# Two 256-token blocks joined into one of 512 in both MLP layers, from block 4 on, with a new order for the head

## The chip, the cores and the metric

The kernel runs on one core of one Trainium2 chip, as one launch. The metric is the device time of that core in microseconds (us); less is better. The median of three runs of the kernel before is 944.13 us.

The engines are named as the profile names them: PE is TensorE (PEld its weight loads), DVE is VectorE, ACT is ScalarE, POOL is GpSimd, SP is the engine that issues the DMAs. "n" in a PE row is the count of columns that stream through it.

## The reference

Attention over keys and values that are averaged in groups of 8, then two matrix products with a rational function between them. 8 sequences of 576 tokens give 4608 rows of 512 features.

```python
k_p = k.reshape(B, H, Sp, 8, D).mean(axis=3)       # B=8, H=8, Sp=72, D=64
v_p = v.reshape(B, H, Sp, 8, D).mean(axis=3)
scores = np.matmul(q, k_p.transpose(0, 1, 3, 2)) / np.sqrt(D)
attn = softmax(scores)
x = np.matmul(attn, v_p)                            # -> (4608, 512)
h = x @ w_in                                        # 512 -> 2048
P = a[0] + a[1]*h + a[2]*h**2 + a[3]*h**3
Q = 1.0 + abs(b[0])*abs(h) + abs(b[1])*h**2
out = (P / (Q + 1e-6)) @ w_out                      # 2048 -> 512
```

The weights come as 64-bit floats and are read as two 32-bit words each.

## The kernel before

**Work.** The 4608 rows are 18 blocks of 256 tokens (`TOK`). The 2048 hidden features are 8 units of 256 (`NU`). For a block, `attend(i)` makes x: scores (tiles `ps`), softmax (`mx`, `e`, `sm`), the transposed probabilities (`am`), and the product with the pooled values (`pv`, in two halves, which ACT copies to x's high part and DVE subtracts to x's low part). `prep_k` and `prep_v` pool the keys and values of a sequence first (`st`, `ks`, `pk`, `pl`, `kpT`; `vs`, `vm`, `vr`; for the first two sequences on PE as `pvs` and `pvr`).

**Each product in three.** Every operand of the two layers is split into a high part and a low part, and a product is high by high, low by high, high by low. For a block and a unit, `mm1` issues 24 matmuls of 256 columns into one PSUM bank `ph`: two halves of the unit's features, three products, four chunks of the 512 features. `rational` turns `ph` into `gh` and `gl` with 13 instructions: ACT `w`, `t`, `r`; POOL `w`; DVE `t` twice (the second is the last reader of `ph`); ACT `rp` twice; DVE `t`, `rp`, `t`; ACT `gh`; POOL `gl`. `mm2` adds 12 matmuls of 512 columns to two banks `po`, one for each half of the block's tokens. PSUM has eight banks, all of one pool: two `po`, the others for `ph`, `rp` (the rational function's scratch) and the attention.

**Weights.** `load_weights` brings 1 MB for a unit of one layer (`rwin`, `rwout`), ACT and DVE rebuild floats from the words in a scratch tile `m`, ACT copies the high part, POOL subtracts the low part. All 16 stay in SBUF. Until unit weights arrive their places hold the first sequences' keys and values (`early`).

**Order.** Nothing runs in the order in which it is written. Each instruction is added to a `Plan` with an engine, a cost and a due time (`plan.now`); `solve` then lists the instructions by a model of engine, port, DMA and buffer times, and `issue` writes them out. Each engine runs its list in order; semaphores make it wait where an operand is late. Where the model sees PE idle, `issue` puts in filler matmuls (256 columns, tile `idle`, or `po<-zero`). Blocks 0 to 3 come first, mixed, while the weights arrive: units 0 to 3 of blocks 0 and 1, all of 2 and 3, then units 4 to 7 of blocks 0 and 1, whose x is written out to HBM (`xd`) and read again. Then block by block, unit by unit. `SHIFTS` are seeds of random offsets on the due times of the first 1850 instructions.

## Time and profile before

| | |
|---|---|
| runs | 943.72, 944.13, 944.32 us |
| span of the profiled execution, first to last instruction | 943.9 us |
| PE, PEld, DVE, ACT, POOL busy | 99%, 90%, 83%, 73%, 56% of the span |
| matmuls `ph` (256 columns), `po` (512 columns) | 3456, 1728 |
| DMA | 75.33 MB, mean 80 GB/s; 275, 313, 390 GB/s in the first three fortieths |
| granted TensorE clock | 1.00 |

The page gives no time of the profiled execution other than its span; the span lies between the lowest and the highest of the three runs, 0.2 us under their median, so a change of the span is taken as a change of the time. A busy share is the time in which an engine had at least one instruction; matmuls overlap, so their own lengths add to more than the span, and the step from one to the next is what they cost.

### The profile page before, as it was taken

What the parts mean: (1) busy time and instruction counts of PE and PEld (TensorE: products, weight loads), DVE (VectorE), ACT (ScalarE), POOL (GpSimd) and SP (SyncE); (2) the same over time, 40 slices, a digit from 0 to 9 for tenths busy, and PEclk for the clock granted to TensorE, in tenths of its full rate; (3) what the DMA queues carried; (4) which work ended last, traced back from release to release, by engine and by line L of the source; (5) the groups of instructions that cost most, each with busy time, mean ns of one, the idle gap of its engine ahead of it and who ended that gap; (6) DMA issues with size and microseconds to landing.
All of it is one profiled execution on the core that took longest, in us unless ns stands there. A gap on an engine that the chain in (4) does not pass through costs nothing.

```text
span 943.9 us, 17079 instructions
## 1 busy us (share of the span) xinstructions
PE 932.3 (99%) x6152; PEld 845.0 (90%) x6152; DVE 786.0 (83%) x1336; ACT 693.7 (73%) x1124; POOL 528.0 (56%) x463
## 2 busy tenths in 40 slices
PE   8899999999999999999999999999999999999998
PEld 8888998989988899998999899998999899999996
DVE  7799988788989888887887997888898987887664
ACT  4788889868675877686776777676868595868674
POOL 4776866866446544445634574447545663544443
PEclk9999999999999999999999999999999999999999
DMA  9994201254235322122603160316222421202000
GB/s 275 313 390 160 45 29 46 67 127 87 49 81 105 86 34 47 29 56 53 138 5 75 51 140 8 54 37 139 47 36 50 97 50 28 51 1 57 1 23 23
DMA packets 185365, 75.33 MB, mean 80 GB/s; under 512 B 162624, under 2 KB 162624, under 8 KB 185280
## 3 DMA queue, kind: packets, MB, share of 16 engines
q1 hardware_dynamic: 185280, 74.23, 31.2%
q8 instruction: 49, 0.80, 0.4%
q14 instruction: 36, 0.29, 0.1%
HBM read 50.60 MB, written 12.58 MB: 67 GB/s over the span
## 4 chain that ended last, share of the span: by engine, by line
PE 87%; DMA 3%; SPq 3%; DVE 3%; POOL 1%; ACT 1%; issue 1%; POOLq 0%; ACTq 0%
PE ph L284 39%; PE po L284 39%; PE pv L284 4%; PE ps L284 4%; SPq L284 3%; DMA q<-in_q_dram 1%; DMA early<-in_v_dram 1%; DVE sm L284 1%; DMA st_v<-in_v_dram 1%; DVE t L284 1%; POOL w L284 0%; PE pvs L284 0%; ACT rp L284 0%; PE pq L284 0%; DVE mx L284 0%
## 5 line engine op out<-in xcount | busy, mean ns | idle before, releaser
L284 PEld LDWEIGHTS ph<-x,win 128*128 128x128 f32 x3264 | 472.7, 188 | 55.5 <-ACT w L284 0.8
L284 PE MATMUL ph<-x,win 128*128 128x256 f32 x3264 | 495.7, 282 | 1.4 <-DVE x L284 0.5
L284 PE MATMUL po<-wout,gh 128*128 128x512 f32 x1152 | 353.1, 397 | 0.1
L284 POOL TENSOR_TENSOR w<-w,r 128x512 f32<-128x512 f32 (+1 forms) x145 | 191.1, 1318 | 230.3 <-ACT r L284 228.1
L284 POOL TENSOR_TENSOR gl<-t,gh 128x512 fp32r<-128x512 f32 (+1 forms) x145 | 193.3, 1333 | 93.1 <-ACT gh L284 91.9
L284 PEld LDWEIGHTS po<-wout,gh 128*128 128x128 f32 x1152 | 185.7, 189 | 12.5 <-POOL wout L284 0.8
L284 PE MATMUL po<-wout,gl 128*128 128x512 f32 x576 | 181.8, 396 | 0.3 <-POOL gl L284 0.3
L284 ACT ACTIVATE rp<-w,cbias 128x512 f32<-128x512 f32 (+1 forms) x145 | 99.6, 687 | 59.8 <-POOL w L284 56.6
L284 DVE SCALAR_TENSOR_TENSOR t<-t,abn,rp 128x512 f32<-128x512 f32 (+1 forms) x145 | 107.3, 740 | 38.4 <-ACT rp L284 35.3
L284 DVE TENSOR_TENSOR t<-t,ph 128x512 f32<-128x512 f32 (+1 forms) x145 | 97.8, 675 | 48.7 <-ACT t L284 46.7
L284 ACT ACTIVATE r<-w,abn 128x512 f32<-128x512 f32 (+1 forms) x145 | 117.9, 813 | 20.8 <-POOL gl L284 11.4
L284 ACT ACTIVATE t<-ph,abn 128x512 f32<-128x512 f32 (+1 forms) x145 | 111.0, 767 | 26.3 <-PE ph L284 23.0
L284 ACT ACTIVATE w<-ph 128x512 f32<-128x512 f32 (+1 forms) x145 | 85.7, 591 | 40.8 <-PE ph L284 34.4
L284 DVE SCALAR_TENSOR_TENSOR t<-t,abn,ph 128x512 f32<-128x512 f32 (+1 forms) x145 | 107.0, 738 | 5.2 <-ACT w L284 1.3
L284 ACT CAST gh<-t 128x512 fp32r<-128x512 f32 (+1 forms) x145 | 88.3, 609 | 20.5 <-DVE t L284 16.9
L284 DVE SCALAR_TENSOR_TENSOR t<-rp,t 128x512 f32<-128x512 f32 (+1 forms) x145 | 99.4, 685 | 4.1
L284 DVE SCALAR_TENSOR_TENSOR rp<-w,rp 128x512 f32<-128x512 f32 (+1 forms) x145 | 99.0, 683 | 0.2
L284 PEld LDWEIGHTS po<-wout,gl 128*128 128x128 f32 x576 | 93.0, 189 | 6.4 <-POOL gl L284 0.5
L284 ACT ACTIVATE rp<-rp 128x512 f32<-128x512 f32 (+1 forms) x145 | 84.1, 580 | 3.6 <-DVE t L284 0.5
L284 POOL TENSOR_TENSOR e<-e,sm 128x576 f32<-128x576 f32 x36 | 41.8, 1175 | 51.2 <-DVE sm L284 38.7
L284 POOL TENSOR_TENSOR st_v<-st_v 128x512 f32<-128x512 f32 (+1 forms) x36 | 36.3, 1015 | 17.4 <-DMA st_v<-in_v_dram 10.7
L284 PE MATMUL ps<-kpT,qT 128*128 128x144 f32 (+1 forms) x320 | 45.6, 292 | 0.4 <-DVE kpT L284 0.2
(101 smaller groups left out, 855.9 us busy)
## 6 DMA issues: line engine op xcount, KB each, us to landing
am<-e SPq DMA_DIRECT2D x224, 48.0 KB, 2.1
out_dram<-ob SPq DMA_DIRECT2D x17, 512.0 KB, 3.1
rwin<-in_moe_w_in_dram SPq DMA_DIRECT2D x8, 1024.0 KB, 11.1
rwout<-in_moe_w_out_dram SPq DMA_DIRECT2D x8, 1024.0 KB, 14.1
st_k<-in_k_dram SPq DMA_DIRECT2D x12, 512.0 KB, 4.8
st_v<-in_v_dram SPq DMA_DIRECT2D x12, 512.0 KB, 4.2
q<-in_q_dram SPq DMA_DIRECT2D x144, 32.0 KB, 2.0
st_v<-in_v_dram SPq DMA_DIRECT2D x48, 64.0 KB, 2.2
```

The lines of the kernel that those rows point to most:

```text
L284: getattr(engines[op.eng], name)(*map(value, args), **{k: value(v) for k, v in kw.items()})
```

## The change

From block 4 on, blocks i and i+1 go through both layers as one of 512 tokens. `mm1_wide` takes one half of a unit's features (128) and both blocks' tokens: 12 matmuls of 512 columns into one bank `ph`. So `u` now counts to 16 for a pair, and `ph`, `t`, `w`, `r`, `gh`, `gl` keep their size. `mm2_wide` adds to four banks `po`, 128 tokens each, instead of two. x lies in one tile `X` with three places for a block; a pair has two of them, and the next pair's first block is attended into the third while the pair runs.

SBUF room for that comes from dropping the pools `stage` and `dec`: weights are decoded in the places of later weights (or in `near` and `far`, two tiles of 1024 columns), and keys, values and outputs are staged in halves of `near` and `far`, so keys, values and outputs move in pieces half as large (769 DMA issues on SP instead of 676; 480 tensor-tensor instructions on POOL instead of 420, 382 on DVE instead of 351). The four and the two coefficients are no longer sent to 128 partitions by DMA; they land on one partition and a matmul (`ab`) spreads them.

The planner's model gets new constants (an engine is free before its result can be read: `TAIL`, `HOP`; lower costs for DVE, ACT and POOL), it tracks parts of tiles through more kinds of views (`box`, `covers`), and instead of random offsets two tables (`LATER`: 154 entries on due times, `HOLD`: 74 earliest starts) shape the order.

```diff
-    LAT = 0.07
+    TAIL = {"sp": 0.0, "pe": 0.16, "pool": 0.06, "dve": 0.09, "act": 0.1}
+    HOP = {"sp": 0.035, "pe": 0.035, "pool": 0.08, "dve": 0.035, "act": 0.035}
...
-    SHIFTS = (600170, 650652, 293686, 721265, 222299, ...
+    LATER = {
+        40: -31199.3, 45: -9979.2, 50: -7560.7, 61: -7094.9, 66: -1347.5, 67: -1073.3,
...
+    HOLD = {
+        71: 22.46, 76: 23.98, 104: 14.67, 116: 22.44, 138: 34.87, 316: 59.14, 458: 31.17, 461: 53,
...
-    dve = Engine(plan, "dve", 0.16, 1.04)
-    act = Engine(plan, "act", 0.17, 0.85)
-    gp = Engine(plan, "pool", 0.45, 1.72)
+    dve = Engine(plan, "dve", 0.068, 1.04)
+    act = Engine(plan, "act", 0.06, 0.85)
+    gp = Engine(plan, "pool", 0.14, 2.15)
...
+    X = new("cpool", "x", [P, 3, 2, NJ, TOK], F32R, "x")
+    near, far = (new("cpool", x, [P, 2 * DM], F32, x) for x in ("in", "out"))
+    taken = {near.tile: 0, far.tile: 0}
+
+    def half(x):
+        n = taken[x.tile] = taken[x.tile] + 1
+        return x[:, n % 2 * DM:(n % 2 + 1) * DM]
...
     def scalars():
-        dma(2, ab[:, 0:4], a.partition_broadcast(P))
-        dma(1, ab[:, 4:6], b.partition_broadcast(P))
+        small("memset", line, 1.0)
         for i in range(4):
-            small("tensor_scalar", out=abn[:, i:i + 1], in0=ab[:, i:i + 1],
-                                scalar1=-WS ** -i, scalar2=None, op0=ALU.mult)
-        act(6).activation(abn[:, 4:6], ab[:, 4:6], AF.Abs)
+            small("memset", scale[:, i:i + 1], -WS ** -i)
+        dma(0.02, ab[:, 0:4], a.unsqueeze(0))
+        dma(0.02, ab[:, 4:6], b.unsqueeze(0))
+        every = bank("ab", [P, 6])
+        pe(220, [mm(every, line, ab, True, True)])
...
-        m = new("dec", "m", [P, CW], F32, f"m_{name}")
+        if u >= NA:
+            m = near if kind == "win" else far
+        else:
+            if kind == "win" and not decoding:
+                decoding.append(new("cpool", "win6", [P, 2 * CW], F32, "m6"))
+            m = (decoding[0] if kind == "win" else early(0, 0))[:, u % 2 * CW:(u % 2 + 1) * CW]
...
+    def slot(i):
+        place_of[i] = i % 2 if i < 4 else (2, 0, 1)[i % 3 - 1]
+        return [X[:, place_of[i], s] for s in range(2)]
...
+    def mm1_wide(i, u):
+        ph = bank(f"ph{i}_{u}", [P, 2, TOK])
+        w, f, n = weights["win", u // 2], u % 2, DM // P
+        lo, hi = sorted((place_of[i], place_of[i + 1]))
+        last = read[-PHS:-PHS + 1] if PHS > 1 else read[-1:]
+        for s, (wi, xi) in enumerate(((0, 0), (1, 0), (0, 1))):
+            last = pe(231.6 * n, [
+                mm(ph, w[:, wi, (2 * c + f) * P:(2 * c + f + 1) * P],
+                   X[:, lo:hi + 1:hi - lo, xi, c, :], s == 0 and c == 0, s == 2 and c == n - 1)
+                for c in range(n)], after=last),
+        return ph
...
+    def mm2_wide(i, u, gh, gl):
+        if u == 0:
+            pos[i] = [bank(f"po{i}_{m}", [P, DM]) for m in range(4)]
+        w = weights["wout", u // 2][:, :, u % 2 * DM:(u % 2 + 1) * DM]
...
+        high, low = ((gh, 0), (gh, 1)), ((gl, 0),)
+        if not final:
+            for terms in (high, low):
+                for m in range(4):
+                    products(m, terms)
+            return
+        tail = last(i, u)
+        for h in range(2):
+            for n in range(2):
+                m = 2 * h + n
+                plan.now += 5.0 * tail
+                products(m, high)
+                products(m, low)
+                row = (i + (h ^ swap)) * TOK + n * P
+                ob = half(near if tail and h else far)
+                evict(n, ob, pos[i][m])
+                dma(256, out[row:row + P, :], ob)
...
-    order += [(i, u) for i in range(4, NBLK) for u in range(NU)]
+    order += [(i, u) for i in range(4, NBLK, 2) for u in range(2 * NU)]
```

What the planner makes of it is seen in the engines' lists. SP's list in the head, first before (the two coefficient loads, `ab`, stand ahead of the second pair of q tiles, `q1`, which tokens 256 to 511 need):

```order
L284 DMA q0_109<-in_q_dram 128x8x64 x2
L284 DMA early0_2_116<-in_v_dram 128x4x512
L284 DMA rwin0_121<-in_moe_w_in_dram 128x4x512
L284 DMA early0_1_103<-in_v_dram 16x2x512 x2
L284 DMA rwin1_145<-in_moe_w_in_dram 128x4x512
L284 DMA ab_177<-in_moe_b_dram 128x2
L284 DMA ab_177<-in_moe_a_dram 128x4
L284 DMA rwout0_214<-in_moe_w_out_dram 128x2x1024
L284 DMA q1_256<-in_q_dram 128x8x64 x2
```

and now (`fourfold` is the tile in which the coefficients land; `early1_2` is the second sequence's values, 1 MB):

```order
L341 DMA early0_2_114<-in_v_dram 128x4x512
L341 DMA rwin0_121<-in_moe_w_in_dram 128x4x512
L341 DMA early0_1_109<-in_v_dram 16x2x512
L341 DMA rwin1_134<-in_moe_w_in_dram 128x4x512
L341 DMA early0_1_109<-in_v_dram 16x2x512
L341 DMA fourfold_140<-in_moe_b_dram 1x2
L341 DMA early1_1_196<-in_k_dram 64x512
L341 DMA rwin2_215<-in_moe_w_in_dram 128x4x512
L341 DMA q1_250<-in_q_dram 128x8x64 x2
L341 DMA rwout1_277<-in_moe_w_out_dram 128x2x1024
L341 DMA early1_2_314<-in_v_dram 128x4x512
```

The 128-row loads of a and b are gone from ahead of `q1`; a third `rwin` stands there in the place of the first `rwout`, with 128 KB of keys.

PE's list in the head, before, from the last transpose of block 0's probabilities (`pr`) to the first product with the values (`pv`); `pq2` transposes a tile of `q1`:

```order
L284 MATMUL pr1_344<-identr_83,e0_240 128x128 x2
L276 MATMUL idle_101<-identr_83 128x256 x22
L284 MATMUL idle_101<-identr_83 128x128
L284 MATMUL pq2_390<-identr_83,q1_256 128x128 x4
L284 MATMUL pv0_0_397<-am0_0_340,vm00_302 128x256
L284 MATMUL pv0_0_397<-am0_0_340,vm10_305 128x256
```

and now, from the product that pools the first values on:

```order
L341 MATMUL pvs0_257<-early0_2_114,identr_76 128x256 x8
L333 MATMUL idle_101<-identr_76 128x256 x16
L341 MATMUL pm0_308<-identr_76,e0_243 128x128 x4
L341 MATMUL pvr0_318<-early0_1_109,fourfold_140 128x128 x8
L341 MATMUL pr0_339<-identr_76,e0_243 128x128 x2
L341 MATMUL pm1_342<-identr_76,e0_243 128x128 x4
L341 MATMUL idle_101<-identr_76 128x128
L341 MATMUL pr1_362<-identr_76,e0_243 128x128 x2
L341 MATMUL pq3_370<-identr_76,q1_250 128x128 x4
L341 MATMUL pv0_0_379<-am0_0_336,vm00_283 128x256
```

The block of 22 fillers before `pq` is gone, 16 stand further up; a transpose of `q1` still stands ahead of the first `pv`.

PE's list in the later part, before, in block 8 (first and second layer alternate, four matmuls of 256 columns and two of 512):

```order
L284 MATMUL ph8_7_5829<-x0_8_5273,win7_1856 128x256 x4
L284 MATMUL po8_0_0_5598<-wout4_1973,gh8_4_5826 128x512
L284 MATMUL po8_0_1_5600<-wout4_1973,gh8_4_5826 128x512
L284 MATMUL ph8_7_5829<-x0_8_5273,win7_1856 128x256 x4
L284 MATMUL po8_0_0_5598<-wout4_1973,gh8_4_5826 128x512
```

and now, where the pair of blocks 8 and 9 ends and that of 10 and 11 begins (the row above this piece is the last `pv11_1`, which makes half of block 11's x):

```order
L341 MATMUL po8_0_5295<-wout7_2036,gl8_15_6180 128x512
L341 MATMUL po8_1_5301<-wout7_2036,gl8_15_6180 128x512
L341 MATMUL po8_2_5304<-wout7_2036,gh8_15_6168 128x512 x2
L341 MATMUL ph10_0_6248<-x_396,win0_332 128x512 x12
L341 MATMUL ph10_1_6273<-x_396,win0_332 128x512 x12
L341 MATMUL ph10_2_6304<-x_396,win1_410 128x512 x4
L341 MATMUL po8_3_5309<-wout7_2036,gh8_15_6168 128x512 x2
L341 MATMUL po8_2_5304<-wout7_2036,gl8_15_6180 128x512
L341 MATMUL po8_3_5309<-wout7_2036,gl8_15_6180 128x512
L341 MATMUL ph10_2_6304<-x_396,win1_410 128x512 x8
L341 MATMUL ph10_3_6339<-x_396,win1_410 128x512 x12
L341 MATMUL po10_0_6372<-wout0_654,gh10_0_6365 128x512 x2
```

Two matmuls of 256 columns have become one of 512, and at a pair's end the first layer of the next pair runs while the last sums of the old one are still open.

More of the change, by code (lines that the diff above doesn't have):

```diff
@@ L54, in box @@
     def box(self):
+        box = [(0, n) for n in self.tile.shape]
+        whole, axes = list(box), list(range(len(box)))
         for name, args, _ in self.chain:
@@ L59, in box, with covers @@
             if name != "__getitem__":
-                return ()
+                break
             idx = args[0] if isinstance(args[0], tuple) else (args[0],)
-            out = []
-            for i, n in zip(idx, self.tile.shape):
-                out.append((i, i + 1) if isinstance(i, int) else
-                           (i.start or 0, n if i.stop is None else i.stop))
-            return tuple(out)
-        return ()
+            left = []
+            for n, d in enumerate(axes):
+                lo, hi = box[d]
+                i = idx[n] if n < len(idx) else slice(None)
+                if isinstance(i, int):
+                    box[d] = lo + i, lo + i + 1
+                else:
+                    left.append(d)
+                    box[d] = (lo + (i.start or 0), hi if i.stop is None else lo + i.stop)
+                    if i.step and i.step > 1:
+                        box[d] = box[d][0], box[d][1] - (box[d][1] - box[d][0] - 1) % i.step
+            axes = left
+        return () if box == whole else tuple(box)
 def meet(a, b):
     return all(x0 < y1 and y0 < x1 for (x0, x1), (y0, y1) in zip(a, b))
+def covers(a, b):
+    return not a or b and all(x0 <= y0 and y1 <= x1 for (x0, x1), (y0, y1) in zip(a, b))
 class Buf:
@@ L230, in solve @@
                 op.end = t + 2 * op.cost
+            op.done = op.end + self.TAIL[op.eng]
             at[op.eng] = op.end
@@ L333, in tile_pooled_attention_then_rational_moe @@
     LAG = 4
+    PHS = 2
     NA = NU // 2
@@ L491, in prep_k @@
         pl = bank(f"pl{n}", [P, P])
-        for c0, c1, np in ((0, 2, P), (2, 4, P), (4, 5, H * SP - 4 * P)):
+        for c0, c1, np in ([(0, 2, P), (2, 4, P)] if n < 2 else [(c, c + 1, P) for c in range(4)]
+                           ) + [(4, 5, H * SP - 4 * P)]:
             nc_ = c1 - c0
@@ L496, in prep_k @@
             else:
-                place = new("stage", "st", [P, 1024], F32, f"st_k{n}_{c0}")[:, 0:nc_ * RW]
+                place = half(near)
             dma(2 * np * nc_, place[:np].rearrange("p (c x) -> p c x", c=nc_),
@@ L562, in prep_v @@
         vrs = vs_all[:, NJ * D:(NJ + 2) * D].rearrange("p (c d) -> p c d", d=D)
-        for c in (2, 0, 1):
-            place = new("stage", "st", [P, 1024], F32, f"st_v{n}_{c}")
-            st = place.rearrange("p (j x) -> p j x", j=2)
-            if c < 2:
-                dma(512, st, rows[2 * c:2 * c + 2, REM:, :].rearrange("j r x -> r j x"))
+        for c in (4, 5, 0, 1, 2, 3):
+            place = half(near)
+            if c < 4:
+                dma(256, place, rows[c, REM:, :])
             else:
@@ L656, in attention @@
         sm = new("work2", "sm", [P, H], F32, f"sm{t}")
+        scores = [bank(f"ps{t}_{c}", [P, 4, SP]) for c in range(2)]
+        calls = [mm(scores[c][r0:r1, 2 * jj:2 * jj + 2, :], qT[:, 2 * c + jj, r0:r1],
+                    kpT[n % 2][:, 2 * c + jj, :], True, True)
+                 for c in range(2) for jj in range(2) for r0, r1, n in sg]
+        for part in [calls] if len(sg) > 1 else [calls[:2], calls[2:]]:
+            pe(1350 if len(sg) > 1 else 244 * 2, part, claims=(e, mx, sm))
         for c in range(2):
@@ L659, in attention @@
             js = slice(2 * c, 2 * c + 2)
-            ps = bank(f"ps{t}_{c}", [P, 4, SP])
-            pe(245 * 2 * len(sg), [
-                mm(ps[r0:r1, 2 * jj:2 * jj + 2, :], qT[:, 2 * c + jj, r0:r1],
-                   kpT[n % 2][:, 2 * c + jj, :], True, True)
-                for jj in range(2) for r0, r1, n in sg], claims=(e, mx, sm))
+            ps = scores[c]
             dve(4 * SP).tensor_reduce(out=mx[:, hs], in_=ps, op=ALU.max, axis=AX.X)
@@ L777, in reload @@
     def reload(i, kept):
-        xs = [new("work2", f"x{s}", [P, NJ, TOK], F32R, f"xr{s}_{i}") for s in range(2)]
+        xs = slot(i)
         for x, d in zip(xs, kept):
@@ L845, in products @@
                 for m in ms], claims=[pos[i][m] for m in ms])
-        if last(i, u):
-            for m in range(2):
-                plan.now += 10.0 * m
-                for n in range(6):
-                    products(n, (m,))
-                ob = new("dec", "m", [P, DM], F32, f"ob{i}_{m}")
-                evict(m, ob, pos[i][m])
-                dma(256, out[i * TOK + m * P:i * TOK + (m + 1) * P, :], ob)
-            return
         for n in range(6):
@@ L915, in tile_pooled_attention_then_rational_moe @@
                 plan.now = due(at)
-        if ("win", u) not in weights:
+        if i < 4 and ("win", u) not in weights:
             load_weights("win", u)
@@ L922, in tile_pooled_attention_then_rational_moe @@
         gh, gl = rational(i, u, ph)
-        if ("wout", u) not in weights:
+        if i < 4 and ("wout", u) not in weights:
             load_weights("wout", u)
```

156 lines of the change are left out of this document (93 added, 63 removed), and 32 rows, old and new, of tables (HOLD, LATER).

## The prediction

> **What bounds the kernel now.** I read the page's first lines, then the busy time by windows, then the chain of work that ended last, PE's waits, and the timelines of PE and SP in the head.
>
> ```profile
> span 943.9 us, 17079 instructions
> PE 932.3 (99%) x6152; PEld 845.0 (90%) x6152; DVE 786.0 (83%) x1336; ACT 693.7 (73%) x1124; POOL 528.0 (56%) x463
> ```
> ```profile
> 0.00:25.00 25.00, 21.66 (x143) 19.76 (x143) 18.12 (x41) 11.22 (x22) 12.08 (x52) 1.00 0.88 264
> 25.00:50.00 25.00, 22.56 (x177) 21.30 (x178) 19.28 (x36) 19.27 (x36) 20.48 (x17) 1.00 1.06 333
> 50.00:75.00 25.00, 24.81 (x172) 22.06 (x172) 22.81 (x40) 21.04 (x33) 17.94 (x10) 1.00 1.04 396
> 500.00:600.00 100.00, 100.00 (x669) 90.56 (x668) 86.18 (x151) 72.33 (x119) 53.95 (x45) 1.00 0.30 67
> ```
>
> The windows (start:end, length, then busy time of PE, PEld, DVE, ACT, POOL, clock, DMA share, GB/s) tell two stages apart. From about 40 us on PE is never without work; the clock is 1.00, DMA is at 0.30. There only fewer or shorter matmuls, or a new wait, can move the end. In the first 50 us the 16 DMA engines are full (0.88, 1.06) and PE has gaps: a start that waits for data.
>
> What a matmul costs is read from unbroken pieces of the chain (start, length, count):
>
> ```profile
> 125.43 1.89 PE ph L284 x16
> 149.82 2.86 PE ph L284 x24
> 174.69 2.38 PE ph L284 x20
> ...
> 227.62 1.83 PE po L284 x8
> ...
> 382.15 1.88 PE pv L284 x16
> ...
> 928.99 11.15 PE po L284 x48
> ```
>
> A `ph` of 256 columns takes 118.1, 119.2, 119.0 ns, together 7.13 / 60 = 118.8; a `po` of 512 columns 228.8 and, over 48, 232.3; a `pv` of 256 columns 117.5.
>
> **The change, part by part.**
>
> *Wide first layer.* Blocks 4 to 17 have 14 x 192 = 2688 `ph` of 256 columns; they become 1344 of 512. Taking a `ph` of 512 columns at the step of a `po`, each saves 2 x 118.8 - 232.3 = 5.3 ns: 1344 x 5.3 = 7.1 us, all on the path. Bounds: by the cheapest 256-column row (`pv`, 117.5) 2.7 ns, 3.6 us; by the dearest `ph` and the cheapest `po` (119.2, 228.8) 9.6 ns, 12.9 us; if the step goes by columns alone, nothing. I take the long `po` row, since it has the new shape and 48 samples. The second layer keeps 1728 `po` of 512 columns: nothing.
>
> [...]
>
> *The head.* PE's list has a transposition of q (`pq`) ahead of the first `pv`; the list now too.
>
> ```profile
> 21.02 2.87 PE L276 MATMUL idle<-identr 128*128 128x256 f32 x22
> 23.73 0.39 PE L284 MATMUL idle<-identr 128*128 128x128 f32 x2
> 25.60 0.63 PE L284 MATMUL pq<-identr,q 128*128 128x128 f32 x4 [1.49 <-DMA q<-in_q_dram]
> ```
> ```profile
> 12.02 13.45 DMA q<-in_q_dram
> ```
> ```profile
> 18.00:20.00 2.00, 2.00 (x19) 1.88 (x19) 1.58 (x4) 0.92 (x4) 1.15 (x1) 1.00 0.63 241
> ...
> 22.00:23.00 1.00, 1.00 (x10) 1.00 (x10) 0.99 (x3) 1.00 (x3) 0.00 (x0) 1.00 0.82 196
> 23.00:24.00 1.00, 1.00 (x10) 0.93 (x8) 0.97 (x2) 1.00 (x3) 0.00 (x0) 1.00 0.44 95
> 24.00:25.00 1.00, 0.12 (x2) 0.00 (x0) 0.97 (x3) 0.31 (x1) 0.61 (x1) 1.00 0.42 62
> ```
>
> PE did 22 fillers and then waited 1.49 us for the second pair of q tiles, which was issued at 12.02 and landed at 25.47. In that stretch the DMA engines were not full: 0.37 x 2 + 0.18 + 0.56 + 0.58 = 2.1 us of their time went unused, around the 128-row loads of `ab`, which stand right ahead in SP's list. Those go; ahead of q now stands the same number of megabytes (a `rwin` for a `rwout`, and 128 KB more). So q should land about 2.1 us sooner, and the gate with it. Bounds: nothing, if the unused time has another cause or block 0's probabilities come later than now; 2.87 + 1.49 = 4.4 us, all fillers and the wait. I take 2.1.
>
> Behind the gate PE waits for small things, up to 100 us:
>
> ```profile
> PE ph L284 <- DVE x L284: 0.5, 1, 0.5
> PE pm L284 <- POOL e L284: 0.4, 1, 0.4
> PE pk L284 <- POOL ks L284: 0.4, 1, 0.4
> PE pv L284 <- DVE am L284: 0.3, 1, 0.3
> ...
> PE pq L284 <- issue: 0.2, 1, 0.2
> ```
> ```profile
> L276 PE MATMUL po<-zero,identr 128*128 128x256 f32 x10 | 1.7, 282 | 0.0
> ```
>
> These four waits and the `pq` make 1.8 us, and ten fillers of 118.8 ns 1.2. The new list puts 40 `ph` between the scores of block 1 and the transposes that need them, where `pm` and `ph` waited, and has no filler in this stretch. But the second sequence's values (`pvs1`) are now wanted some 7 us after the gate, when their 1 MB, issued behind 8 MB, has hardly landed at the 333 to 396 GB/s above. I take half of the waits and the fillers: 0.9 + 1.2 = 2.1 us less. Bounds: 3.0 less, 2 more.
>
> *The end.* Before, the last unit's `ph` was written and read by halves in one bank:
>
> ```profile
> 926.79 0.74 PE L284 MATMUL ph<-x,win 128*128 128x256 f32 x4 [0.39 <-ACT w L284]
> ...
> 928.25 0.74 PE L284 MATMUL ph<-x,win 128*128 128x256 f32 x4 [0.25 <-ACT t L284]
> ```
>
> A wide `ph` is read only when whole: these waits, 0.6 us, go. After it stand 48 `po` as before. Output stays two 256 KB pieces at the end: nothing.
>
> *New waits between pairs.* At a pair's start nothing of its own can fill PE until the first `gh` is there. Its chain, by the means of the groups:
>
> ```profile
> L284 ACT ACTIVATE w<-ph 128x512 f32<-128x512 f32 (+1 forms) x145 | 85.7, 591 | 40.8 <-PE ph L284 34.4 <-DVE t L284 6.1
> L284 ACT ACTIVATE r<-w,abn 128x512 f32<-128x512 f32 (+1 forms) x145 | 117.9, 813 | 20.8 <-POOL gl L284 11.4 <-DVE rp L284 1.9
> L284 POOL TENSOR_TENSOR w<-w,r 128x512 f32<-128x512 f32 (+1 forms) x145 | 191.1, 1318 | 230.3 <-ACT r L284 228.1 <-PE ph L284 1.6 <-PE ps L284 0.7
> L284 ACT ACTIVATE rp<-w,cbias 128x512 f32<-128x512 f32 (+1 forms) x145 | 99.6, 687 | 59.8 <-POOL w L284 56.6 <-DVE am L284 0.9 <-DVE kpT L284 0.8
> L284 ACT ACTIVATE rp<-rp 128x512 f32<-128x512 f32 (+1 forms) x145 | 84.1, 580 | 3.6 <-DVE t L284 0.5
> L284 DVE SCALAR_TENSOR_TENSOR t<-t,abn,rp 128x512 f32<-128x512 f32 (+1 forms) x145 | 107.3, 740 | 38.4 <-ACT rp L284 35.3 <-DVE t L284 0.5
> L284 DVE SCALAR_TENSOR_TENSOR rp<-w,rp 128x512 f32<-128x512 f32 (+1 forms) x145 | 99.0, 683 | 0.2
> L284 DVE SCALAR_TENSOR_TENSOR t<-rp,t 128x512 f32<-128x512 f32 (+1 forms) x145 | 99.4, 685 | 4.1
> L284 ACT CAST gh<-t 128x512 fp32r<-128x512 f32 (+1 forms) x145 | 88.3, 609 | 20.5 <-DVE t L284 16.9 <-PE ph L284 2.9
> L284 ACT ACTIVATE t<-ph,abn 128x512 f32<-128x512 f32 (+1 forms) x145 | 111.0, 767 | 26.3 <-PE ph L284 23.0 <-DVE rp L284 2.4 <-POOL w L284 0.5
> L284 DVE TENSOR_TENSOR t<-t,ph 128x512 f32<-128x512 f32 (+1 forms) x145 | 97.8, 675 | 48.7 <-ACT t L284 46.7 <-ACT w L284 1.7
> L284 DVE SCALAR_TENSOR_TENSOR t<-t,abn,ph 128x512 f32<-128x512 f32 (+1 forms) x145 | 107.0, 738 | 5.2 <-ACT w L284 1.3
> ```
>
> The first nine add to 6.7 us. Behind one other unit on ACT (its six instructions, 4.0 us) it is 10.7. At the start of pair 10 the list has 36 `ph` and 4 `po` between the end of `ph10_0` and the first use of its `gh`, 40 x 232.3 ns = 9.3 us; the like places at other pairs' starts and ends, by the same count, have 8.2 (the end of the first pair) to 18 us. So each of the six transitions loses between nothing and about 2 us, 0 to 12 in all. I take 0.3 each, 1.9 us, near the lower end, because a chain that meets a free engine is nearer to 6.7; and the nine fillers that the list has at the end of the first pair, 1.1. Sum 3.0.
>
> *At nothing:* the third place in `X` (block i+2's x is copied while the pair still runs; if it comes late, `ph` of the next pair waits for it, behind it all of PE); 93 more issues on SP and 60 more instructions on POOL, since POOL is busy 56% and keys and values are pooled a pair ahead (if that cover is gone, `kpT` is late and `ps` waits); weights decoded in one or two scratch places (the units that use them come later than their landing).
>
> **The sum.** 943.9 - 7.1 - 2.1 - 2.1 - 0.6 + 3.0 = 935.0 us of span. The median of the runs is 0.2 above the span: 935.2.
>
> **The rivals.**
>
> *Too few banks (slower).* Four banks now hold `po`, so four are left for `ph`, `rp`, `ps` and `pv`, where there were six. A `ph` bank is free when DVE has read it twice: 0.591 + 0.813 + 0.767 + 0.675 + 0.738 = 3.6 us after the last matmul when ACT does `r` before `t`, and 4.8 with two more instructions of 0.6 us ahead (the next x is copied at that time). In 16 places of the list a `ph` begins 2.8 to 4.2 us, 3.5 on average, after the end of the one two before it (pair 10: 12 x 232.3 = 2.8). If that bank is the only one, a place loses 4.8 - 3.5 = 1.3 us: 20 us, 955. From 0.7 us a place the kernel is slower. For it: PE's list has nothing else there. Against: at those places the old pair's four sums are just being given back, so a third bank is often free.
>
> *The head gains nothing:* full DMA engines (1.06) or a later transposition set the gate anyway. 935.2 + 2.1 + 2.1 = 939.4. For it: the shares of 1.04 to 1.06 up to 75 us.
>
> *A smaller fixed cost per matmul:* by the `pv` row 3.6 in place of 7.1 us, 938.7. [...] By columns alone the first layer saves nothing: 942.3.
>
> *More is gained:* transitions lose only the fillers (1.9 less) and the gate moves by 4.4 (2.3 less): 931.0.
>
> **How the numbers follow.** Forecast 935.2, chance 0.52, its own range 933 to 938; head without gain 0.15; smaller fixed cost 0.10; more gained 0.13; columns alone 0.03; banks 0.07. About 0.2% of the time, 1.9 us, is what can be told from no change. The first four are faster: 0.90. Columns alone, and the mild part of the banks, within 0.2%: 0.04. Slower: 0.06. From 930.5 to 941 lie the forecast, the small fixed cost, nearly all of the head and half of the gains: 0.82.
>
> **What would show it.** Right: chain pieces of the new `ph` near 232 ns; `pq` or the first `pv` at about 23.5 us; no `DMA q` wait of 1.5; windows from 100 us on with PE within 0.3 us of full per 50; no waits of `ph` for ACT at the end. Wrong: waits of PE `ph` for DVE `t` or of `po` for ACT `gh` that sum to over 8 us at the pairs' starts (banks or transitions); a `ph` of 237 ns; `pq` still at 25.6.

## The result, and the profile after

The changed kernel takes 954.71 us (median of four runs, 953.26 to 956.76) against 943.98 for the kernel before in the same job: a ratio of 1.0115 [1.0101, 1.0128], 10.7 us slower, where 8.9 us less was forecast. The device time lies 1.7 us above the span for runs of before and 1.9 for runs of after, not 0.2: by this difference the profiled execution of before, with its span of 943.9 us, took some 945.6 us, more than any of the four runs of before (943.72 to 944.32).

The page of after opens with these lines (compare the 932.3 us of PE in 6152 matmuls before):

```profile
span 954.8 us, 14586 instructions
PE 932.8 (98%) x4796; PEld 776.1 (81%) x4796; DVE 778.0 (81%) x1367; ACT 695.5 (73%) x1124; POOL 535.9 (56%) x532
```

Busy time by windows of after (start:end, length, PE, PEld, DVE, ACT, POOL, clock, DMA share, GB/s):

```profile
25.00:50.00 25.00, 24.89 (x185) 24.27 (x186) 21.34 (x39) 20.58 (x34) 17.13 (x14) 0.93 1.06 358
500.00:600.00 100.00, 97.81 (x465) 78.56 (x464) 86.74 (x158) 70.31 (x114) 53.10 (x54) 1.00 0.32 67
```

The second 25 us are now nearly full (24.89 us of PE; 22.56 before), at a mean clock of 0.93. In the steady stretch from 500 to 600 us PE lacks 2.2 us where it lacked nothing. Much of the loss is in the part without a data wait.

The chain of work that ended last (page, part 4, shares of the span), before:

```profile
PE 87%; DMA 3%; SPq 3%; DVE 3%; POOL 1%; ACT 1%; issue 1%; POOLq 0%; ACTq 0%
```

and after:

```profile
PE 45%; DVE 22%; ACT 9%; SPq 7%; POOL 6%; issue 5%; DMA 5%; DVEq 0%; ACTq 0%; POOLq 0%
```

PE carried 87% of the chain; now it carries 45%, and 37% runs through VectorE, ScalarE and GpSimd (5% before), although their busy shares did not rise (83, 73 and 56% before; 81, 73 and 56% now).

Both kernels issue the same 1728 `po` with `wout`. I cut each run at the start of the 48th, the 384th and the last of them: the head (s1), the rest of the weights' arrival and of blocks 0 to 3 (s2), the steady part (s3). Windows of the tile `wout`, before (columns as above, without DVE):

```profile
0.00:83.10 83.10, 13.43 (x48) 8.22 (x48) 3.16 (x3) 7.16 (x3) 1.00 0.98 323
83.10:256.00 172.90, 92.05 (x338) 57.67 (x336) 5.20 (x5) 12.02 (x5) 1.00 0.25 61
256.00:940.10 684.10, 409.11 (x1346) 212.81 (x1344) 0.00 (x0) 0.00 (x0) 1.00 0.25 55
```

and after:

```profile
0.00:84.20 84.20, 12.76 (x48) 8.36 (x48) 4.20 (x4) 8.10 (x4) 0.98 0.92 294
84.20:263.10 178.90, 95.06 (x338) 56.75 (x336) 4.18 (x4) 11.10 (x5) 1.00 0.32 78
263.10:951.10 688.00, 344.14 (x1346) 247.88 (x1344) 0.00 (x0) 0.00 (x0) 1.00 0.24 52
```

The head is 1.1 us longer, the second stretch 6.0, the third 3.9. (In the text s3 is 0.3 less, since it ends at the start of the last `po`.) With each matmul put at the median step of its kind (the time from its start to the next one's), the stretches divide so (us); what is above the median counts as lost:

| | s1 work, fillers, lost | s2 | s3 |
|---|---|---|---|
| before | 62.4, 14.7, 4.1 | 171.0, 0.2, 1.7 | 678.9, 0.0, 4.9 |
| after | 65.5, 11.4, 5.2 | 170.9, 0.0, 8.0 | 669.4, 1.5, 17.0 |

Work fell by 6.5 us and fillers by 2.0; lost time rose by 19.5; together +11.0, which is what PE's end moved (939.7 to 950.7). The line between work, fillers and lost time is a convention: drawn in other ways, single entries move by several us, and the rise of lost time in s3 lies between 8 and 14 us. Work also moved between the stretches: s1 now holds 256 matmuls of attention and pooling in place of 220, s3 488 in place of 513. So s3 by itself is a fair measure only between kernels with nearly the same matmuls in it. The wide matmuls did become cheaper. The question is where the lost time comes from.

The waits of PE from 256 to 951 us (us in total, times, longest), before and then after:

```profile
PE ph L284 <- ACT w L284: 0.4, 1, 0.4
PE pv L284 <- DVE am L284: 0.4, 1, 0.4
PE po L284 <- POOL gl L284: 0.3, 1, 0.3
PE ph L284 <- ACT t L284: 0.3, 1, 0.3
PE ps L284 <- DVE kpT L284: 0.2, 1, 0.2
```
```profile
PE ph L341 <- ACT w L341: 1.7, 2, 1.4
PE ps L341 <- ACT w L341: 1.4, 1, 1.4
PE ps L341 <- DVE e L341: 1.0, 1, 1.0
PE pv L341 <- DVE e L341: 0.9, 1, 0.9
PE pv L341 <- DVE t L341: 0.9, 1, 0.9
PE ph L341 <- DVE t L341: 0.7, 2, 0.5
PE ps L341 <- DVE t L341: 0.5, 2, 0.3
PE ph L341 <- DVE kpT L341: 0.4, 1, 0.4
PE po L341 <- ACT gh L341: 0.3, 1, 0.3
PE pv L341 <- DVE am L341: 0.3, 1, 0.3
```

1.6 us became 8.1; the rest of the lost time, some 5.6 us of the rise in s3, has no named wait. All but the last two rows, 0.6 us, are of a kind of which before has 0.7: `ps` does not read `w`, nor `pv` read `e`. Such a matmul waits for the bank that it is to write, until the last reader of the tile that was there is done. Those bank waits went from 0.7 to 7.5 us.

### The profile page after: what moved, and what is told of

Its sections match the earlier page's. It is cut to its first block, busy times and chain, and to the rows that moved or that the text cites. A ratio compares the mean times of both kernels' runs of the same rounds, so it can differ in the third digit from the quotient of the medians.

```text
span 954.8 us, 14586 instructions
## 1 busy us (share of the span) xinstructions
PE 932.8 (98%) x4796; PEld 776.1 (81%) x4796; DVE 778.0 (81%) x1367; ACT 695.5 (73%) x1124; POOL 535.9 (56%) x532
## 4 chain that ended last, share of the span: by engine, by line
PE 45%; DVE 22%; ACT 9%; SPq 7%; POOL 6%; issue 5%; DMA 5%; DVEq 0%; ACTq 0%; POOLq 0%
PE ph L341 21%; PE po L341 19%; DVE t L341 9%; SPq L341 7%; PE pv L341 3%; ACT rp L341 3%; POOL w L341 3%; DVE rp L341 2%; DVE am L341 2%; ACT t L341 2%; DVE e L341 2%; PE ps L341 2%; DMA q<-in_q_dram 2%; POOL gl L341 2%; DVE in L341 1%
## 5 line engine op out<-in xcount | busy, mean ns | idle before, releaser
L341 PE MATMUL ph<-x,win 128*128 128x512 f32 (+1 forms) x2112 | 445.0, 355 | 5.6 <-DMA x<-xd 2.7
L341 PEld LDWEIGHTS ph<-x,win 128*128 128x128 f32 x2112 | 354.6, 188 | 74.0 <-issue 4.1
L341 PE MATMUL po<-wout,gh 128*128 128x512 f32 x1152 | 320.8, 398 | 1.7 <-ACT gh L341 1.6
L341 PEld LDWEIGHTS po<-wout,gh 128*128 128x128 f32 x1152 | 209.0, 188 | 46.9 <-ACT gh L341 3.8
L341 PE MATMUL po<-wout,gl 128*128 128x512 f32 x576 | 177.8, 400 | 0.2 <-POOL gl L341 0.2
L341 PEld LDWEIGHTS po<-wout,gl 128*128 128x128 f32 x576 | 104.9, 188 | 23.7 <-POOL gl L341 1.1
L341 ACT ACTIVATE rp<-rp 128x512 f32<-128x512 f32 (+1 forms) x145 | 84.1, 580 | 3.0
L341 POOL TENSOR_TENSOR in<-in 128x256 f32<-128x256 f32 (+2 forms) x82 | 50.6, 624 | 7.2 <-DMA in<-in_v_dram 4.5
L341 PE MATMUL pv<-am,vm 128*128 128x256 f32 (+3 forms) x288 | 48.1, 284 | 2.5 <-DVE e L341 0.9
```

The source lines that it names most:

```text
L341: getattr(engines[op.eng], name)(*map(value, args), **{k: value(v) for k, v in kw.items()})
```

## The experiments

The letters in the expectations: A, the wide layer itself brings the waits, A1 because fewer banks are free, A2 because the order has less slack; B, what came with it does; S and T, in later runs, the staging in halves and the third x place. All runs, with s1, s2, s3 of the profiled one, and the ratio to before in the same job:

| run | median us | ratio [95%] | s1, s2, s3 |
|---|---|---|---|
| before | 943.98 | 1 | 83.1, 172.8, 683.8 |
| after | 954.71 | 1.0115 [1.0101, 1.0128] | 84.1, 178.9, 687.7 |
| e1_narrow | 953.97 | 1.0105 [1.0088, 1.0122] | 82.4, 179.0, 685.6 |
| e2_head_table | 974.49 | 1.0324 [1.0309, 1.0339] | 82.3, 182.4, 703.3 |
| e3_parked | 950.89 | 1.0070 [1.0056, 1.0084] | 82.2, 173.1, 689.5 |
| e4_less_dve | 947.87 | 1.0036 [1.0023, 1.0050] | 84.0, 177.5, 682.1 |
| e5_after_tick | 957.39 | 1.0141 [1.0122, 1.0160] | 85.4, 178.6, 687.5 |
| e6_before_tick | 944.15 | 0.9997 [0.9988, 1.0007] | 82.3, 172.8, 683.4 |
| e7_reload_moved | 958.72 | 1.0154 [1.0139, 1.0170] | 83.1, 180.3, 687.9 |
| e8_narrow_stage | 946.93 | 1.0031 [1.0019, 1.0044] | 82.3, 175.0, 685.0 |
| e9_far_head | 1038.26 | 1.1001 [1.0985, 1.1018] | 85.2, 182.0, 765.3 |
| e10_wide_best | 952.80 | 1.0099 [1.0083, 1.0114] | 85.8, 178.1, 681.7 |
| e11_far_best | 1010.55 | 1.0718 [1.0691, 1.0744] | 91.4, 174.0, 739.7 |
| e12_warm | 954.69 | 1.0112 [1.0096, 1.0128] | 83.3, 177.7, 687.0 |
| e13_wide_re | 952.00 | 1.0084 [1.0071, 1.0097] | 83.6, 178.7, 682.2 |
| e14_stage_re | 945.77 | 1.0018 [1.0009, 1.0027] | 86.8, 174.3, 678.8 |
| e15_stage_re_warm | 945.14 | 1.0010 [1.0001, 1.0018] | 86.5, 174.6, 677.6 |
| e16_narrow_parked | 953.63 | 1.0101 [1.0085, 1.0117] | 81.8, 179.5, 686.5 |
| e17_four_places | 978.75 | 1.0371 [1.0343, 1.0399] | 89.9, 180.4, 703.0 |
| e18_three_places | 971.93 | 1.0294 [1.0276, 1.0312] | 90.0, 188.7, 686.0 |

### Without the width, and without the late part of the tables

`e1_narrow` is the changed kernel with the blocks apart again; the tables keep what precedes block 4.

```diff
-    order += [(i, u) for i in range(4, NBLK, 2) for u in range(2 * NU)]
+    order += [(i, u) for i in range(4, NBLK) for u in range(NU)]
```

> Everything of the change is kept (third place of x, decode places, new costs, the two tables for the operations before block 4) but the width: blocks 4 to 17 are done one by one with two sums each, as before, and the tables have no entries behind block 4's start. Theory A (the loss is the width's: with four banks for the sums TensorE waits for banks from 240 us on, 9.8 us of not being busy in 240:930 against 1.5 before): not busy in 240:930 falls to 1 to 3 us, the 5.6 us that width saved are given back, time 943 to 951. Theory B (the loss is that of the other parts, the head, the reload and the new places): not busy in 240:930 stays near 10 and the time is 955 to 962.

`e2_head_table` keeps the width, and its `LATER` and `HOLD` stop where those of `e1_narrow` do.

> The wide kernel, with the entries of the two tables for operations from block 4 on taken out (numbers 1366 and up); the entries before stay. Theory A1 (four free banks are too few in any order): the waits from 240 us on stay or grow, 954 to 965. Theory A2 (the tables made an order without room, in which each late eviction or quotient step is a wait of TensorE): the order without them has more room, 940 to 950.

Without the width (and without its late table entries) the kernel is as slow as with it, 953.97 us, between the ranges given for A and for B, and s2 is the same 179.0: most of the 10 us is there without the width. But under the same short tables the width costs 20.5 us more (974.49, above both of its ranges). Windows of the filler's tile `zero` (PE, PEld, DVE, clock, DMA share, GB/s), first `e2_head_table`, then `e1_narrow`:

```profile
265.00:968.00 703.00, 16.00 (x122) 14.96 (x122) 0.00 (x0) 1.00 0.23 50
```
```profile
261.00:947.00 686.00, 0.00 (x0) 0.00 (x0) 0.00 (x0) 1.00 0.25 55
```

The wide order without its late table has 122 fillers in the steady part, the narrow one none. So that table does not take the slack: it wins 20 us back, and this part of A2 falls.

### Fewer free banks

`e3_parked` is the kernel before with two banks held from block 4 to shortly before the end; `e16_narrow_parked` is `e1_narrow` with the same. The planner lists both anew, so the order changes with the banks.

```diff
+    parked = [bank(f"parked{n}", [P, 2, P]) for n in range(2)]
...
+    for at in order.index((4, 0)), len(order) - 4:
+        plan.now = due(at)
+        for x in parked:
+            plan.add("pe", 0, [mm(x[:, 0], ident, ident, True, True)], early=0.0)
```

> The kernel before, narrow throughout, in which two more PSUM banks hold nothing from block 4's start to shortly before the end, so that its blocks work in two banks of sums and four others, as the wide pairs do. Theory A1 (four free banks are too few in themselves): TensorE gets 5 to 11 us of new waits in 240:930 and the time is 949 to 955. Theory A2 (four do where the order leaves room): 943.5 to 947.

> The narrow kernel of the first experiment (954.0 us, no table entries from block 4 on) with two PSUM banks that hold nothing from block 4 to shortly before the end: it has four free banks beside its two sums, as the wide kernel without such entries has (974.5 us). Theory A1 (the number of free banks makes the 20.5 us between the two): 965 to 975. Theory T (the pair does: at its end the first layer's work is used up, and the next pair's cannot begin until its second block's x is there): 954 to 961.

In before the two banks cost 6.5 us, most of it in s3 (689.5 against 683.8), as A1 has it. In the narrow kernel they cost nothing: 953.63 against 953.97. Its PE waits from 265 to 960 us:

```profile
PE ps L305 <- DVE kpT L305: 1.6, 2, 0.9
PE pv L305 <- DVE am L305: 0.9, 2, 0.5
PE ph L305 <- DVE t L305: 0.6, 1, 0.6
PE ph L305 <- DVE e L305: 0.4, 1, 0.4
```

The first two read what they wait for; bank waits are 1.2 us (0.2 of them not shown). Four banks beside those of `po` are left there, as many as in the wide kernel, and the order does with them. The number of banks is not enough as a cause.

### The chain to a bank's release

`e4_less_dve` leaves out one multiplication of the quotient's chain (VectorE's `t` by `ph`, 0.68 us) from block 4 on. `e5_after_tick` and `e6_before_tick` keep all steps and put a memset of 32 columns behind the step after it, the last reader of `ph`, in after and in before.

```diff
+        if wide:                                   # e4: the multiplication is not issued
+            plan.left_out.add(len(plan.ops) - 2)
...
+        if wide:                                   # e5 (in e6 the same instruction)
+            plan.ticks.add(read[-1].seq)
...
+            if op.seq in self.ticks:
+                self.nc.vector.memset(self.tick, 0.0)
```

> The changed kernel, with the same order on every engine, in which one of VectorE's steps of the quotient (t = t times h) is left out in blocks 4 to 17: 112 instructions of 0.69 us, 77 us of VectorE's work, none of it TensorE's; so the polynomial lacks a factor there. Theory A (TensorE waits because VectorE and ScalarE release banks and finish gh late in an order without room): not busy in 240:930 falls from 9.8 us to 2 to 5, time 946 to 950. Theory C (the gaps are TensorE's own, from the form of its instructions or the clock): unchanged within 1 us, 953 to 956.

> The changed kernel, same order, with one more instruction on VectorE (a memset of 128x32 to a place nobody reads, some 0.1 us) behind the second step of each quotient in blocks 4 to 17: 113 of them, about 11 us of VectorE's work among 778 us. Theory A (an order without room: each late step of VectorE is a later release of a bank, and TensorE waits): 5 to 12 us slower than the changed kernel's 954.7, so 960 to 967. Theory C (the waits have another cause and VectorE has room): 954 to 957.

> The kernel before with the same added instruction at the same step, 113 times. VectorE is as busy there (578 of 690 us in 240:930), so load alone would tell no difference. Theory A (before has room in its order): 0 to 2 us slower than 944.0, at most 946. Theory D (every order of this work is this sensitive): 5 to 12 us slower here too, 949 to 956.

One step less, in the same order, takes 5.6 us from s3 (687.7 to 682.1), 6.8 in all; the bank waits of PE from 256 to 951 us fall from 7.5 to 3.8. 113 memsets change s3 by -0.2 us in after and -0.4 in before. The profiled runs of `e5_after_tick` and after differ by 0.8 us, and its mean clock was 0.77 from 20 to 25 us and 0.54 from 25 to 30 where after's was 1.00 and 0.66, which is some 6.9 us at 0.5 against 3.4; its median is 2.7 us higher, at clocks of 0.996 to 0.998, and the expected 960 to 967 was missed. This fits a kernel that feels the length of the chain from `ph` to its last reader. It does not rule out VectorE's load: the memsets stand behind that last reader and add, by my estimate, at most 113 x 0.165 = 19 us of work (the one memset of VectorE in after, 128x128, took 0.165 us; these have 32 columns), while the step left out spares 113 x 0.68 = 77. The chain of work in `e4_less_dve`:

```profile
PE 71%; DVE 12%; ACT 5%; SPq 4%; DMA 3%; issue 3%; POOL 2%; DVEq 0%; POOLq 0%; ACTq 0%
```

PE has 71% of it again, and VectorE 12 in place of 22.

### The second stretch: one reload, and the staging

In after, one wait makes 2.7 of the 6 us of s2. SP's issues (start, length) and PE's row:

```profile
195.68 0.55 SPq L341 DMA_DIRECT2D x<-xd  x1
...
197.57 0.61 SPq L341 DMA_DIRECT2D x<-xd  x1
```
```profile
203.50 1.18 PE L341 MATMUL ph<-x,win 128*128 128x256 f32 x8 [2.68 <-DMA x<-xd]
```

The two 512-KB reloads land 4.4 and 5.8 us after their issue, and PE arrives first. `e7_reload_moved` issues them right behind the last instruction that they depend on:

```diff
+        for late in [o for o in order if o.seq in self.RELOAD]:      # 1148, 1149
+            order.remove(late)
+            at = max(n for n, o in enumerate(order) if o in late.deps) + 1
+            order.insert(at, late)
```

> The changed kernel with one move: the two loads that bring block 1's x back stand in SyncE's queue right behind the last use of that place, ahead of the loads for block 4's heads that they stood behind; every other instruction in its order. The 2.7 us wait of TensorE at 200.4 us should go. If it is paid in full: 951.5 to 952.5. If what it hides comes up behind it, or the order soon waits for VectorE as before: 953 to 955.

The wait is gone, but at the same place PE now waits for the quotient (waits from 155 to 240 us):

```profile
PE po L346 <- ACT gh L346: 2.3, 1, 2.3
```

s2 is 180.3 us, no gain: the reload was only the last of several things that were late. The mean clock of this profiled run is 0.998, and 1.00 from 15 to 50 us: by my estimate 0.002 x 955.4 = 1.9 us were lost to it, and even if all of that lay in s2, s2 without it would be 178.4, still no real gain. The median, 958.72, is above both expected ranges, at clocks of 0.994 to 0.998.

`e8_narrow_stage` is `e1_narrow` with two staging places of 4 KB, two x places, and keys and values in whole pieces again (72 fewer DMA issues on SP, 60 fewer tensor-tensor instructions on POOL). The outputs still go in halves.

```diff
-    X = new("cpool", "x", [P, 3, 2, NJ, TOK], F32R, "x")
+    X = new("cpool", "x", [P, 2, 2, NJ, TOK], F32R, "x")
+    pool("stage", 2)        # [P, 1024], for prep_k and prep_v
```

> The narrow kernel of the first experiment (954.0 us) with one more thing put back: x has two places again, and the 8 KB per partition so freed hold the two 4 KB places of staging through which keys and values of later heads come, as in the kernel before (the changed kernel brings them through two halves of 2 KB, in 11 loads more for each head). Between the 48th and the 384th product of wout (83 to 261 us) the narrow kernel lost 9.6 us to waits and fillers, the kernel before 1.9. Theory S (the small staging pays for x's third place: later loads, a longer queue on SyncE, late steps behind them): that falls to 2 to 5 us, time 945 to 950. Theory P (the order from the new costs is to blame, whatever the staging): 952 to 956.

This gives 7.0 us back by the medians (953.97 to 946.93). The profiled runs differ by 4.7 us, 4.0 of them in s2; that of `e8_narrow_stage` ran at a mean clock of 0.996 (0.83 from 20 to 30 us), that of `e1_narrow` at 0.998. PE's waits in s2, first `e1_narrow`, then `e8_narrow_stage`:

```profile
PE po L305 <- ACT gh L305: 2.0, 2, 1.4
PE po L305 <- POOL gl L305: 0.8, 1, 0.8
```
```profile
PE ps L305 <- DVE t L305: 1.1, 1, 1.1
```

The staging of keys and values in halves, which pays for x's third place, with the orders that it brings, is the largest single part found (S).

### More banks by moving `rp`

`e9_far_head` puts the quotient's scratch `rp` of most units into SBUF (`far`), under the tables of `e2_head_table`; `e11_far_best` does so with a table of its own.

```diff
-        rp = bank(f"rp{i}_{u}", [P, 2, TOK])
+        rp = (half(far).rearrange("p (f t) -> p f t", f=2) if i >= 4 and 3 <= u < 2 * NU - 1
+              else bank(f"rp{i}_{u}", [P, 2, TOK]))
```

> The wide kernel without table entries from block 4 on (974.5 us), with one edit: rp, the quotient's scratch, lies in the two halves of the output's SBUF place in units 3 to 14 of each pair, and no longer in a PSUM bank. Nothing is left out. Theory A1 (banks are what is short): with about 0.8 of a bank fewer held at a time the waits of blocks 4 to 17 fall by half, 955 to 966. Theory L (the length of the quotient's chain or late loads set the pace): 970 to 977, and since rp in SBUF can slow VectorE beside GpSimd, perhaps a little more.

> As the kernel before this one in the call, with its own such table, and rp in the output's SBUF place in units 3 to 14 as in the experiment on banks. Theory A1: 3 to 8 us below the one with rp in PSUM, 934 to 942. Theory A2 (order alone): within 2 us of it.

Both are far slower, far outside every expected range, and it says nothing on banks, because the steps themselves grew, and because the two places of `far` are shared with the outputs. VectorE's three steps with `rp` (count, busy, mean ns, idle before) in `e2_head_table`, and those of `e9_far_head` with `rp` in SBUF (there named `out`):

```profile
L305 DVE SCALAR_TENSOR_TENSOR t<-t,abn,rp 128x512 f32<-128x512 f32 x105 | 77.8, 741 | 49.4 <-ACT rp L305 49.0
L305 DVE SCALAR_TENSOR_TENSOR rp<-w,rp 128x512 f32<-128x512 f32 x105 | 71.9, 685 | 0.1
L305 DVE SCALAR_TENSOR_TENSOR t<-rp,t 128x512 f32<-128x512 f32 x104 | 71.0, 683 | 1.8
```
```profile
L305 DVE SCALAR_TENSOR_TENSOR t<-t,abn,out 128x512 f32<-128x512 f32 x71 | 68.2, 961 | 22.5 <-ACT out L305 22.4
L305 DVE SCALAR_TENSOR_TENSOR out<-w,out 128x512 f32<-128x512 f32 x71 | 68.7, 968 | 3.8 <-DVE t L305 0.5
L305 DVE SCALAR_TENSOR_TENSOR t<-out,t 128x512 f32<-128x512 f32 x71 | 76.5, 1077 | 1.3
```

2.1 us became 3.0 in a unit, on the quotient's chain.

### Other orders, and fillers in the head

`e10_wide_best` (costs of DVE, ACT and POOL in the model 0.088, 0.08 and 0.16, `HOLD` empty) and `e13_wide_re` (after's own costs and `HOLD`) are the changed kernel with another `LATER`, in `e13_wide_re` from 50 us on. `e14_stage_re` is `e8_narrow_stage` with such a table.

> The wide kernel with all its parts, and another order: 0.02 us more is assumed for each instruction of VectorE, ScalarE and GpSimd, and the tables are replaced by one of shifts chosen so that the end moves little when instructions run late. Theory A2 (it is the order that has no room; width with four banks pays where the order has some): 938 to 947. Theory A1 (four banks are too few in any order): 952 or more.

> The wide kernel with the changed kernel's head (the order up to 50 us) and its costs, and new shifts for what comes later, chosen so that late instructions move the end less. Theory A2 (order): the stretch from 84 to 263 us falls by 2 to 4 us from 178.9, the one behind it from 688.0 to 677 to 683, time 943 to 949. Theory A1 (four banks lose what width saves, in any order): the last stretch stays at or above the 684 of the kernel before, time 949 to 954.

> The narrow kernel with the staging of before (946.9 us), with new shifts chosen in the same way behind 50 us. Nothing is left out. If the small staging, the width's banks and the order are what cost, this keeps only what the change has of gains (the head, the costs): 937 to 942, below the kernel before by 2 to 7 us, with its runs spread by the clock. If the new costs and head bring nothing by themselves: 943 to 947.

The other wide orders bring s3 down to 681.7 and 682.2, 5.5 to 6.0 us below after's with nearly the same matmuls in it. That is also below before's 683.8, but some work of before's s3 is done in s1 there; s1 and s3 together are 767.5 and 765.8 against 766.9, so a saving by the wide layer of more than 1 us is not shown. The totals, 952 to 953, lie in the ranges given for A1, the s3 of `e13_wide_re` in that for A2: neither is settled. The first has a head 1.7 us longer than after's, the second as much more behind the last `po`, and both keep an s2 of 178 to 179. `e14_stage_re` comes to 945.77, no better than before.

`e12_warm` puts nine fillers ahead of two late transposes of the head, `e15_stage_re_warm` the same into `e14_stage_re`. Without them the granted clock fell in the head of after, to a mean of 0.66 from 25 to 30 us.

```diff
+        self.warm = dict(zip((order[n] for n in late), (5, 4)))      # ahead of pr, of pq
...
+                for _ in range(self.warm.get(op, 0)):
+                    self.nc.tensor.matmul(self.idle.ap(), lhsT=self.filler, start=True, stop=True,
+                                          rhs=self.filler.unsqueeze(1).to_broadcast([128, 2, 128]))
```

> The changed kernel, with nine more fillers (matmuls of 256 columns to the tile idle, 0.12 us each) in the head: five ahead of the transposition pr and four ahead of pq, where TensorE stood idle at 23.5 to 24.1 and 24.6 to 25.1 us; the instruction that gives idle's bank back stands behind them. Theory K (these gaps let the granted clock fall to 0.5 for 3.4 us, a loss of 1.7 us in the profiled run and more in others): every run at a clock of 0.999 to 1.000, 951.5 to 953.3. Theory N (the clock falls for another reason, the transpositions or what comes later): clocks 0.996 to 0.999 as before, 953 to 957.

> As the kernel ahead of it in the call, with the nine fillers in the head. Theory K: 1 to 3 us below it, clocks of 0.999 to 1.000, 935 to 940. Theory N: the same as it within 1 us.

Windows of all engines (columns as in the first windows), after, then `e12_warm`:

```profile
25.00:30.00 5.00, 4.89 (x29) 4.90 (x30) 4.38 (x7) 3.46 (x5) 0.00 (x0) 0.66 0.97 381
```
```profile
25.00:30.00 5.00, 4.97 (x43) 4.77 (x42) 4.90 (x9) 4.57 (x9) 0.62 (x1) 1.00 0.92 356
```

A mean of 0.66 over 5 us is 3.4 us at half clock. With the fillers it stays at 1.00 and PE does 43 matmuls instead of 29, some of them fillers. In the profiled run PE ends 2.7 us sooner, but the median hardly moves (954.69 against 954.71; 945.14 against 945.77). One of the four runs of `e12_warm` still had 0.996, and the slowest, 957.07 us, had 1.000: for the time this is inconclusive.

### Places for x

`e17_four_places` gives x four places, so that a pair never shares one with the pair ahead; `e18_three_places` is the same kernel with three. Both have only the head's part of the tables, other due times for the attention, and leave out the `wout` weights of unit 3 (unit 2's are used).

```diff
-        place_of[i] = i % 2 if i < 4 else (2, 0, 1)[i % 3 - 1]
+        place_of[i] = i % 2 if i < 4 else i % 2 + 2 - i // 2 % 2 * 2
```

> The wide kernel with four places for x in place of three, so that both blocks of the next pair can be attended while a pair runs, and with their due times set earlier (the first block 8 units ahead of its pair, the second 10 us). The room is made by leaving out unit 3 of the second layer's weights: it is not loaded or decoded, and its products use unit 2's. No table entries behind the head's. Theory T: few fillers (po<-zero, 151 of them in the wide kernel without entries) and a last stretch (behind the 384th product of wout) 8 us or more shorter than with three places. Theory A1: within 4 us of three places, since the banks are as few.

> The same with three places, everything else as in the kernel with four, unit 3's weights left out too. Theory T: 8 to 15 us slower than four places, the loss in fillers and waits at the pairs' ends. Theory A1: within 4 us.

Windows of the filler's tile, `e17_four_places` and then `e18_three_places`:

```profile
270.00:973.00 703.00, 0.61 (x4) 0.60 (x4) 0.00 (x0) 1.00 0.23 51
```
```profile
278.00:965.00 687.00, 6.02 (x47) 5.64 (x47) 0.00 (x0) 1.00 0.23 52
```

Four places take the fillers away, 47 to 4, and yet the kernel is 6.8 us slower; PE's longest wait in the steady part is now this:

```profile
PE pv L305 <- DVE am L305: 6.6, 4, 2.8
```

T falls in its total (s2 and s3 together 883.4 against 874.7), and 6.8 us is outside A1's 4 us as well. `e18_three_places` has an s3 of 686.0 where `e2_head_table`, with the same places but other due times and longer tables, has 703.3. Most of that is no gain: its s1 and s2 are 14.0 us longer, and more of the first layer stands in them (s2 holds 360 matmuls' worth of 512 columns of `ph` against 332). The totals differ by 2.6 us.

## Why the prediction was wrong, by its own steps

The forecast of the span was -8.9 us, the end of PE moved by +11.0: 20 us apart. They divide into 1.5 (the wide `ph`), 2.0 (the head), 6.1 (second stretch) and 11.2 (third), less 0.9 of other work. The step that failed is the term for new waits: behind the head the sum had only those at the pairs' starts, and put everything else there at nothing.

- *The wide `ph`, -7.1.* Right in kind, somewhat large. Pieces of after's chain (start, length, count):

```profile
425.20 2.73 PE ph L341 x12
...
430.72 2.79 PE ph L341 x12
...
436.32 3.74 PE ph L341 x16
```

  9.26 / 40 = 231.5 ns a step; the median over all is 232 against twice 118 (interpolated 232.2 and 118.2), so some 4.2 ns x 1344 = 5.6 us, inside the bounds of 3.6 to 12.9. "By columns alone" is excluded. The 1728 `po`, put at nothing, rose at the median from 231.2 to 232.3 ns, some 1.9 us, which is counted in the other work.
- *The head, -2.1 and -2.1.* Of the 4.2 us about half was gained, and not in the way that was forecast; that it is the size of one term is luck. Fillers and lost time in s1 fall from 18.8 to 16.6, by 2.2, while 3.1 us more work is done there. But the gate hardly moved: the second q tiles were issued 1.0 us later, at 13.04, and landed at 25.06 us in place of 25.47, and PE waited for them again, to 25.11 and not to the forecast 23.5 (timeline of after):

```profile
25.11 1.11 PE L341 MATMUL pq<-identr,q 128*128 128x128 f32 x4 [0.53 <-DMA q<-in_q_dram]
```

  The gain is fewer fillers, and a clock of 0.5 for 3.4 us took, by my estimate, 3.4 x 0.5 = 1.7 back. (PE was also not quite "never without work" from 40 us on: it has 24.81 and 24.63 of 25 us in the two windows from 50 to 100.)
- *The end, -0.6.* The time lost in the last pair fell from 1.5 to 0.4 us: right within half a microsecond.
- *New waits between pairs, +3.0.* This step failed, not in what it priced but in what it left out. The priced parts came to 1.8: fillers 1.5, and 0.3 of `po` for `gh` at a pair's start (six transitions at 0.3 are 1.8, not the 1.9 of the sum). But fillers and lost time in s3 went from 4.9 to 18.5, +13.6. The largest named part, 6.8, is banks given back late, mostly in the second half of the pairs, for which the sum had no term.
- *"At nothing".* This step failed too. The 93 more issues, the smaller pieces on POOL and the shared staging were said to be covered because POOL is busy 56%; undoing the staging of keys and values gave 4.0 us in s2 and 7.0 by the medians.
- *The rival "too few banks"* named the kind of wait and had a chance of 0.07. That its 955 meets the measured time is luck: it put 20 us on such waits, where 6.8 more are named, and 6.1 of the loss lie in s2. Its reason, the count of banks, holds in `e3_parked` and not in `e16_narrow_parked`. Nearer to the runs is that the chain to a bank's release meets an order without room: one step less in it gives 5.6 us of s3, another order as much. This is argued, since the step left out also spares VectorE 77 us.

Undone one after the other from after: the width with its late table entries 0.7 us, the staging 7.0, leaving 2.9 over before (head, costs and tables; `e14_stage_re` and `e15_stage_re_warm` leave 1.7 and 1.1). These shares belong to these orders, since each of these kernels is listed anew: under the short tables the width costs 20.5. What stays open is which property of the wide layer makes its orders wait. Its matmuls are 5.6 us cheaper in every one, and over six wide orders (after and `e2`, `e10`, `e13`, `e17`, `e18`) s3 runs from 681.7 to 703.3 us. It was not shown that a wide order with the old staging exists that beats before; that kernel was not run, and none of those run is faster than before.

## What to carry to other kernels

A matmul made cheaper is worth its step only while the order leaves room around it: multiplying the saving by the count is the safe half of the sum, and the chain that frees each bank, with what stands between it and the next use, is the other half. What a change moves "at no cost" (staging places, smaller pieces, a queue's list) should be undone by itself on the chip before the headline edit is blamed or praised. Cutting two runs at the same instruction and dividing each stretch into work, fillers and lost time shows in one table where a loss sits, which shares of busy time do not; count the instructions in each stretch as well, since work that moved over a cut looks like a gain.
